# One fused attention and MLP kernel: every queue planned anew with other engine and load times

## The chip, the cores and the metric

The kernel runs on one core of one Trainium2 chip. A core has five instruction queues that matter here: PE (TensorE, the matrix engine, whose weight loads the profile lists apart as PEld), DVE (VectorE), ACT (ScalarE), POOL (GpSimd) and SP (SyncE, which here issues nearly all DMAs). The metric is the device time of one execution in microseconds (us). Before the change the median of three runs was 362.16 us, the lowest 360.83 and the highest 362.58.

## The reference

The first half is a linear attention without a softmax. For each of 8 batches and 8 heads, with 576 positions and 64 features:

```python
kv  = einsum('bhsd,bhse->bhde', k, v)
out = einsum('bhsd,bhde->bhse', q, kv)
rms = sqrt(mean(out*out, axis=-1) + 1e-06)
x   = out / rms * g_norm              # heads side by side: (8, 576, 512)
```

The second half is an MLP block with two mixings, over positions ("tok") and over channels ("ch"), the latter with 2048 hidden units:

```python
a1  = alpha1 * x + beta1
u   = x + lam * einsum('ts,bsd->btd', w_tok, a1)
a2  = alpha2 * u + beta2
out = u + lam * (maximum(a2 @ w_ch1, 0) @ w_ch2)
```

Inputs and output are float32.

## The kernel before

All work is written down as a list of operations and then put in order by a planner inside the kernel file. `P.op(engine, cost, fn, r, w)` notes one operation: its engine (or several engines with a cost for each), a cost in us, the function that issues its instructions, and the keys that it reads and writes, from which dependences follow. Loads and stores are operations of SP with a second figure, `dma_us`, for the transfer.

The stages of one batch b are these, and the names return in the text:

- the product kv(b) on PE: L666 (batch 0 and from batch 2 on), L760 and L770 (batch 1);
- the splitting of q into two bf16 parts (L536 and L621) and its transposition, by PE (L644) for batch 1 and by DMA from batch 2 on; batch 0 is transposed in float32 (L693, L707);
- qkv(b), the second product and its normalisation: L858 for batch 0, L431, L851 and L951 later, then ACT's square (L888), DVE's sum, reciprocal and multiplication (L890, L896, L909), and the input of the next stage, `rt` and, for positions 512 to 575, `rtt` (L915, L981). POOL multiplies x by g for the first two batches (L936, L995);
- tok(b): L1095 for batch 0, L1018, L1049 and L1070 later, then DVE's sum into `xm` (L1031, L1057, L1112);
- ut(b), the transposed input of the channel stage, `a2t`: by PE (L1130) with the evacuations L1139 on ACT and L1140 on DVE for the first two batches, by DMA from batch 2 on;
- ch1(b) on PE (L1181, L1196, L1208 or L1223) with the relu on ACT (L1170, L1171) into `ht`;
- ch2(b) on PE (L1272 and, for the last chunk, L1253), DVE's sum (L1282) and the store.

Beside batches 0 and 1 the weights come in: w_tok is transposed on PE (L1414, L1428), w_ch1 is cast to bf16 and w_ch2 multiplied by lam (L1505). The first loads on SP are chained, so that they are issued in the order in which the program names them.

The planner (`schedule`) simulates five queues. At each moment an idle queue takes the operation of highest priority whose dependences have ended and for which a PSUM bank is free. An operation holds its engine for its cost; what depends on it may start 0.35 us after the end for PE, 0.15 us after it for the others. All loads share one transfer resource (`dma_free`): each takes `dma_us` of it and has landed 2.0 us later. POOL operations and DVE operations marked `port` exclude one another. An operation with costs for two engines goes to the one that would finish it sooner.

As long as the first product of ch1(0) has not started, an idle PE is given fillers: matmuls of zeros (L1586), which keep PE active. Due times are set for the products of ch1(0) and ch2(0) and for the first of ch1(1); `hasten` turns them into priorities for all that these depend on, counted back along the costs. `plan` repeats this for 8 rounds with priorities that are taken backward from the plan before, keeps the best and then shakes its priorities with a list of seeds, each of which moves a random part of them. All other operations keep the priority of their place in the program.

The result is a fixed order on every queue. On the chip nothing is chosen any more: each engine works through its list and waits on semaphores where an operation depends on another queue. The planner's times are not in the program; only the order that follows from them is.

Of the kernel before, what the change touches and what calls it, by code (L numbers as in the profile page):

```python
# [11 lines left out]
ACT = mybir.ActivationFunctionType  # L12
# [37 lines left out]
class Prog:  # L50
# [134 lines left out]
    def schedule(self):  # L185
# [91 lines left out]
        while left:  # L277
            progressed = False
            for e, q in queues.items():
                while q and free[e] <= t + 1e-9:  # L280
                    pick = None
                    first = self.warm and self.warm[0].start is None
                    cands = q[:self.pe_window] if e == "PE" and not first else q[:400]
                    for o in cands:
                        if not ready(o, t):
                            continue
                        if takes_port(o, e) and port_free > t + 1e-9:
                            continue
                        if isinstance(o.eng, tuple) and better_elsewhere(o, e, t):
                            continue  # L290
                        if e in ("ACT", "DVE", "POOL") and sooner(o, e, t):
                            continue
                        pick = o
                        break
                    if pick is None and e == "PE" and first:

                        pick = self.op("PE", 0.43 if t < 6.1 else 0.22, lambda e: self.warm[1](e, self.warm[3]),
                                       r=self.warm[2], w=[self.warm[3]])
                        if ready(pick, t):
                            left += 1  # L300
                            q.append(pick)
                        else:
                            self.ops.remove(pick)
                            self.warm[3].ops.remove(pick)
                            self.lastw.pop(self.warm[3])
                            if self.warm[3].ops:
                                self.lastw[self.warm[3]] = [self.warm[3].ops[-1]]
                            pick = None
                    if pick is None:
                        break  # L310
                    if isinstance(pick.eng, tuple):
                        for e2 in pick.eng:
                            queues[e2].remove(pick)
                        pick.eng, pick.cost = e, pick.cost[e]
                    else:
                        q.remove(pick)
                    for tile in pick.alloc:
                        tile.bank = place(tile, t)
                        for b in range(tile.bank, tile.bank + tile.n):
                            if owner[b] is not None:  # L320
                                pick.deps.update(owner[b].ops)
                            owner[b] = tile
                    pick.start = t
                    free[e] = t + pick.cost
                    if takes_port(pick, e):
                        port_free = free[e]
                    if pick.lat is not None:
                        dma_free = max(dma_free, t + 0.6) + pick.lat
                        pick.end = dma_free + 2.0
                    else:  # L330
                        pick.end = t + pick.cost + (0.35 if e == "PE" else 0.15)
                    order[e].append(pick)
                    events.add(pick.end)
                    events.add(free[e])
                    left -= 1
                    progressed = True
# [100 lines left out]
def bass_transnormer_attn__then__resmlp_affine_kernel(  # L437
# [15 lines left out]
    with ExitStack() as stack:  # L453
# [85 lines left out]
        def load_main(tile, key, src, b, hs, eng="SP"):  # L539
            P.op(eng, 0.6, lambda e: e.dma_start(  # L540
                tile[:, hs].rearrange("p h c d -> p h (c d)"),
                src[b, hs, 0:512, :].rearrange("h (p c) d -> p h (c d)", c=4)),
                w=[(key, a) for a in range(hs.start // 4, hs.stop // 4)],
                dma_us=4.0 * (hs.stop - hs.start) / 8)

        def load_tail(tile, key, src, b, lo, eng="SP"):
            P.op(eng, 0.6, lambda e: e.dma_start(
# [8 lines left out]
        def load_first(a):  # L556
            for key, src, tile in (("kf", k, kf), ("vf", v, vf)):
                P.op("SP", 0.6, lambda e, src=src, tile=tile: e.dma_start(
                    nine(tile, 0, a).rearrange("p x c d -> p x (c d)"),
                    src[0, 4 * a:4 * a + 4].rearrange("(x y) (p c) d -> (y p) x (c d)",  # L560
                                                      y=2, c=9)),
                    w=[(key, a)], dma_us=1.55)

        def load_first_tail(a):
            for y in range(2):
                P.op("SP", 0.45, lambda e, y=y: e.dma_start(
                    qft[0:64, 4 * a + 2 * y:4 * a + 2 * y + 2, :],
                    q[0, 4 * a + y:4 * a + y + 3:2, 512:576, :].rearrange("h s d -> s h d")),
                    w=[("qft0", a, y)], dma_us=0.25)

        def load_kv(b):
            j = (b + 1) % 2
            for tile, src, n in ((kf, k, "kf"), (vf, v, "vf")):
                if b > 1:
                    P.op("SP", 0.6, lambda e, src=src, tile=tile: e.dma_start(
                        tile[:, j].rearrange("p (z f) -> p z f", z=4),
                        src[b].rearrange("(z y) (p c) d -> (y p) z (c d)", y=2, c=9)),
                        w=[(n, j)], dma_us=3.1)
                    continue
                P.op("SP", 0.6, lambda e, tile=tile, src=src: e.dma_start(  # L580
                    rows512(tile).rearrange("p h c d -> p h (c d)"),
                    src[b, :, 0:512, :].rearrange("h (p c) d -> p h (c d)", c=4)),
                    w=[(n, j)], dma_us=3.4)
                for g in range(2):
                    P.op("SP", 0.5, lambda e, tile=tile, src=src, g=g: e.dma_start(
                        rows64(tile)[64 * g:64 * g + 64],
                        src[b, 4 * g:4 * g + 4, 512:576, :].rearrange("h s d -> s h d")),
                        w=[(n + "t", g)], dma_us=0.4)

        def load_q(b, hs=ALL[0], tails=True):  # L590
            load_main(qf, "qf", q, b, hs)
# [32 lines left out]
        def qt_dma(b):  # L624
# [10 lines left out]
            for a, hs in enumerate(HALVES):  # L635
                for cs in PAIRS:
# [3 lines left out]
                    def f(e, cs=cs, t=t, hs=hs, n=n):  # L640
                        for h in range(4):
                            for i, c in enumerate(cs):
# [5 lines left out]
                    P.op("PE", 0.25 * n, f, r=["identb"] + [x for c in cs  # L648
                                                           for x in keys_of(c, (a,))], w=[t])
                    P.op(act_dve(512 * n, 1.5), 0, lambda e, cs=cs, t=t, hs=hs, n=n: copy(  # L650
                        e, qt[:, hs, 128 * cs[0]:128 * cs[0] + 128 * n],
# [91 lines left out]
        def kv_groups(b):  # L743
# [10 lines left out]
            def main(a):  # L754
                ts.append(P.ptile(1))

                def f(e):
# [6 lines left out]
                P.op("PE", 1.1, f, r=[("kf", buf), ("vf", buf)], w=[ts[a]])  # L764

            def tails():
                def f(e):
# [64 lines left out]
        def qkv_groups(b):  # L832

            def group(cs, hs):
# [33 lines left out]
                         + ([("q32", h0 // 2), ("q32", h0 // 2 + 1)] if cs[0] < 4  # L868
                            else [("q32t", h0 // 4)]), w=[t])
                else:  # L870
                    P.op("PE", 0.059 * m + 0.03, f,
                         r=[("qt", c, a) for c in cs for a in aa]
                         + [("kvd", a, h, i) for a in aa for h in range(2) for i in range(3)],
                         w=[t])
# [64 lines left out]
            def tail():  # L939
# [7 lines left out]
                def f(e):  # L947
# [9 lines left out]
                P.op("PE", 0.3, f, r=[("qt", 4, a) for a in range(2)] + KVD, w=[t])  # L957
# [53 lines left out]
        def tok_groups(b):  # L1011
            def group(cs):
                t = P.ptile(len(cs))
                scs = 5 if b < MIX else 4
                for i, c in enumerate(cs):
                    def f(e, i=i, c=c):
                        for sc in range(scs):
                            m = e.matmul(t.ap()[:, i, :], tok_w(sc, c), rsrc(b, sc),  # L1018
                                         start=(sc == 0), stop=(sc == 4))
                        return m  # L1020
                    P.op("PE", 0.217 * scs, f,
                         r=[kk for s in range(scs) for kk in wtk(s) + rkeys(b, s)], w=[t])
                if b < MIX:
                    finish(cs, t)
# [142 lines left out]

        def ch1_groups(b):
            def relu(t, src, dst, fj, n):
                o = P.op("ACT", act_us(n) + 0.09, lambda e: e.activation(  # L1170
                    dst, src(), ACT.Relu, bias=hb[:, fj:fj + 1]) if b > 1 else e.activation(  # L1171
                    dst, src(), ACT.Relu), r=[t, ("hb", fj)] if b > 1 else [t], w=[("ht", fj)])
                mark(b, 0, fj + 1.5, o)
# [195 lines left out]
        for i, hs in enumerate(HALVES):  # L1369
# [4 lines left out]
            wst, moe_w_tok[0:512, :].rearrange("(p c) s -> p c s", c=4)),  # L1374
            w=["wst"], dma_us=3.45)
        P.op("SP", 0.6, lambda e: e.dma_start(wst2, moe_w_tok[512:576, :]),
             w=["wst2"], dma_us=0.6)
        P.chain = False

        wz_op = P.op("DVE", 0.3, lambda e: e.memset(wz.bitcast(mybir.dt.uint32), 0), w=["wz"])  # L1380
# [23 lines left out]
        def wt_groups():  # L1404
# [3 lines left out]
            def group(sc):  # L1408
# [3 lines left out]
                def f(e):  # L1412
# [67 lines left out]
        def load_w(i):  # L1480
# [6 lines left out]
            if i < 4:  # L1487
                P.op("SP", 0.6, lambda e: e.dma_start(
                    s_, moe_w_ch1[:, 512 * i:512 * i + 512].rearrange(
                        "(j p) f -> p j f", p=128)), w=sk, dma_us=2.75)  # L1490
# [95 lines left out]
            return e.matmul(t.flat(), wz[:, 0:128], wz, start=True, stop=True)  # L1586
# [33 lines left out]
```

## Time and profile before

| what | us |
|---|---|
| median of three runs | 362.16 |
| the profiled execution | 360.87 |
| its span, from the first to the last instruction | 359.1 |
| PE busy | 353.5 |
| DVE busy | 239.7 |
| ACT busy | 158.3 |
| POOL busy | 25.9 |
| first product of ch1(0) starts (L1196) | 34.70 |
| first product of ch1(1) starts (L1223) | 78.22 |

The profile shows one execution. Times in its views count from the start of the span. "PE L1272 x28" in a timeline means 28 instructions of line 1272, merged. In the chain that ended last, each step is either work or a wait, named after what ended it. "Busy" means that an instruction was under way on the engine; its successor may start before it ends. The mean granted TensorE clock was 1.000.

### The profile page before, as it was taken

The numbers are of one execution on the slowest core, as the hardware profiler recorded it, in microseconds if no ns is written. First come the engines' busy times: TensorE is split into PE (matmuls) and PEld (weight loads), VectorE is DVE, ScalarE is ACT, GpSimd is POOL, SyncE is SP. The second block draws the span as 40 slices with busy tenths as digits, with TensorE's granted clock in tenths as the row PEclk, the third lists the DMA queues.
The fourth block names the chain that finished last, engine by engine and source line by source line (L and its number), as shares of the span: only waits on it lengthen the run. The fifth ranks groups of instructions, "written<-read, shape, count | busy, mean of one in ns | idle before, by whom it ended". The sixth has DMA issues, their size and how long they took to land.

```text
span 359.1 us, 7676 instructions
## 1 busy us (share of the span) xinstructions
PE 353.5 (98%) x3470; PEld 202.7 (56%) x3246; DVE 239.7 (67%) x356; ACT 158.3 (44%) x274; POOL 25.9 (7%) x31
## 2 busy tenths in 40 slices
PE   8999999989999999999999999999999999999996
PEld 4888464477644654457644654457654554457644
DVE  4388989987884389865995388865996378830021
ACT  2365894047730386018730287017740186007600
POOL 4145024400000000000000000000000000000000
PEclk9999999999999999999999999999999999999999
DMA  7999999599066950589536960387026510140022
GB/s 266 354 356 373 405 409 375 177 230 339 5 88 170 288 203 1 104 149 274 210 79 172 264 235 2 88 157 223 6 58 166 101 31 0 53 131 8 2 58 88
DMA packets 79896, 60.15 MB, mean 168 GB/s; under 512 B 53037, under 2 KB 63541, under 8 KB 79736
## 3 DMA queue, kind: packets, MB, share of 16 engines
q1 hardware_dynamic: 79840, 59.67, 56.9%
q8 instruction: 26, 0.43, 0.5%
q14 instruction: 6, 0.05, 0.0%
q10 hardware_dynamic: 24, 0.01, 0.0%
HBM read 38.82 MB, written 9.44 MB: 134 GB/s over the span
## 4 chain that ended last, share of the span: by engine, by line
PE 97%; DMA 1%; DVE 1%; SPq 0%; issue 0%
PE ps L1272 34%; PE ps L1223 20%; PE ps L1181 15%; PE ps L1018 7%; PE ps L666 5%; PE ps L851 2%; PE ps L431 2%; PE ps L858 1%; PE ps L1049 1%; DMA vf<-in_v_dram 1%; PE ps L1095 1%; PE ps L693 1%; PE ps L1253 1%; PE ps L1130 1%; PE ps L1070 1%; PE ps L951 1%
## 5 line engine op out<-in xcount | busy, mean ns | idle before, releaser
L1272 PE MATMUL ps<-w,ht 128*128 128x512 bf16 x560 | 126.1, 379 | 0.0
L1170 ACT ACTIVATE ht<-ps,hb 128x512 bf16<-128x512 f32 (+1 forms) x96 | 70.9, 740 | 43.2 <-PE ps L1223 33.6
L1272 PEld LDWEIGHTS ps<-w,ht 128*128 128x128 bf16 x560 | 53.2, 98 | 63.1 <-issue 2.0
L1223 PE MATMUL ps<-a2t,w 128*128 128x320 bf16 (+1 forms) x512 | 72.6, 299 | 1.0 <-DVE a2t L1140 1.0
L1223 PEld LDWEIGHTS ps<-a2t,w 128*128 128x128 bf16 x512 | 49.4, 98 | 21.8 <-ACT a2t L1139 1.3
L1181 PE MATMUL ps<-a2t,w 128*128 128x512 bf16 x240 | 54.5, 379 | 0.0
L728 ACT ACTIVATE kvd<-ps 64x128 bf16<-64x128 f32 x24 | 6.5, 272 | 102.8 <-PE ps L666 102.7
L1282 DVE TENSOR_TENSOR xm<-ps,xm 128x512 f32<-128x512 f32 x31 | 21.0, 687 | 26.3 <-PE ps L1272 26.1
L1181 PEld LDWEIGHTS ps<-a2t,w 128*128 128x128 bf16 x240 | 22.6, 98 | 25.4
L890 DVE TENSOR_REDUCE small<-sq 128x16 f32<-128x1024 f32 (+2 forms) x20 | 20.5, 1027 | 18.9 <-ACT sq L888 18.7
L1018 PE MATMUL ps<-rt,wt 128*128 128x512 bf16 x112 | 25.8, 379 | 0.0
L1171 ACT ACTIVATE ht<-ps 128x512 bf16<-128x512 f32 (+1 forms) x32 | 19.9, 653 | 4.5 <-DVE hb L537 2.8
L1031 DVE TENSOR_TENSOR xm<-ps,xm 128x1024 f32<-128x1024 f32 x14 | 17.1, 1220 | 5.4 <-PE ps L1070 5.4
L909 DVE TENSOR_TENSOR xm<-ps,small 128x1024 f32<-128x1024 f32 (+1 forms) x18 | 19.8, 1105 | 0.6
L888 ACT ACTIVATE sq<-ps 128x1024 f32<-128x1024 f32 (+2 forms) x20 | 17.5, 873 | 5.2 <-PE ps L858 3.6
L733 DVE TENSOR_TENSOR kvd<-ps,kvd 64x128 bf16<-64x128 f32 x24 | 6.9, 288 | 18.3 <-ACT kvd L728 18.1
L666 PEld LDWEIGHTS ps<-vf,kf 64*64 64x64 f32 x1008 | 15.9, 135 | 5.3 <-issue 3.4
L1018 PEld LDWEIGHTS ps<-rt,wt 128*128 128x128 bf16 x112 | 10.9, 98 | 12.9 <-issue 0.4
L666 PE MATMUL ps<-vf,kf 64*64 64x64 f32 x1008 | 17.7, 221 | 0.1
L621 DVE TENSOR_TENSOR qs<-qf,qs 128x1024 bf16<-128x1024 f32 x13 | 16.5, 1297 | 0.3 <-ACT qs L536 0.3
L1282 DVE TENSOR_TENSOR xtl<-ps,xtl 128x512 f32<-128x512 f32 x4 | 2.8, 691 | 20.2 <-PE ps L1272 20.1
L1037 DVE TENSOR_TENSOR a2b<-xm,a_bc 128x512 bf16<-128x512 f32 x24 | 15.5, 688 | 0.4
(136 smaller groups left out, 347.1 us busy)
## 6 DMA issues: line engine op xcount, KB each, us to landing
out_dram<-xm SPq DMA_DIRECT2D x31, 256.0 KB, 3.1
qf<-in_q_dram SPq DMA_DIRECT2D x7, 1024.0 KB, 7.2
kf<-in_k_dram SPq DMA_DIRECT2D x6, 1152.0 KB, 7.8
vf<-in_v_dram SPq DMA_DIRECT2D x6, 1152.0 KB, 12.2
stg<-in_moe_w_ch_dram SPq DMA_DIRECT2D x3, 1024.0 KB, 14.5
kf<-in_moe_w_ch_dram SPq DMA_DIRECT2D x2, 1024.0 KB, 12.5
kf<-in_k_dram SPq DMA_DIRECT2D x2, 576.0 KB, 5.1
vf<-in_v_dram SPq DMA_DIRECT2D x2, 576.0 KB, 6.0
```

Source lines behind the costliest of these rows:

```text
L666: m = e.matmul(t.ap(slice(64 * x, 64 * x + 64))[:, y, 0:64], nine(kf, b, a)[r, x, c, :], nine(vf, b, a)[r, x, c, :], start=(c == 0), stop= ...
L888: P.op("ACT", act_us(64 * m), lambda e: e.activation(sqv, raw(), ACT.Square), r=[t], w=[("sq", sqs)])
L890: P.op("DVE", dve_us(64 * m), lambda e: e.tensor_reduce(out=smv, in_=sqv.rearrange("p (h d) -> p h d", h=m), axis=AX.X, op=ALU.add), r=[(" ...
L909: P.op("DVE", dve_us(64 * m), lambda e: e.tensor_tensor(out=x3, in0=split(raw()), in1=inv, op=ALU.mult), r=[t, ("sm", sms)], w=xk, pri=-200)
L1018: m = e.matmul(t.ap()[:, i, :], tok_w(sc, c), rsrc(b, sc), start=(sc == 0), stop=(sc == 4))
L1031: P.op("DVE", dve_us(512 * n), lambda e: e.tensor_tensor(out=x, in0=t.ap(rows) if n > 1 else t.flat(rows), in1=x, op=ALU.add), r=[t] + xk, ...
L1170: o = P.op("ACT", act_us(n) + 0.09, lambda e: e.activation(dst, src(), ACT.Relu, bias=hb[:, fj:fj + 1]) if b > 1 else e.activation(dst, sr ...
L1171: dst, src(), ACT.Relu, bias=hb[:, fj:fj + 1]) if b > 1 else e.activation(
L1181: m = e.matmul(t.flat(), w, a2t[:, dj, 0:512], start=(dj == 0), stop=(dj == 3))
L1223: m = e.matmul(t.ap()[:, i, 0:n], w1[:, dj, 128 * fj:128 * fj + 128], a2t[:, dj, 320 * i:320 * i + n], start=(dj == 0), stop=(dj == 3))
L1272: m = e.matmul(t.flat(), ht[:, fj, 128 * c:128 * c + 128], w2[:, fj, :], start=(fj == 0), stop=(fj == 15))
L1282: P.op("DVE", dve_us(512), lambda e: e.tensor_tensor(out=x, in0=t.flat(), in1=x, op=ALU.add), r=[t] + keys, w=keys)
```

## The change

Only numbers of the planner change, in four kinds: the time after which ACT and DVE are free again, the landing times of loads, the costs of some operations on PE and ACT, and the seeds. What is computed, the engines that may do it and the buffers stay as they are; every queue's order is planned anew from the new numbers.

```diff
 # schedule(): fillers, free times, landings
-  pick = self.op("PE", 0.43 if t < 6.1 else 0.22, lambda e: self.warm[1](e, self.warm[3]),
+  pick = self.op("PE", 0.38 if t < 5.9 else 0.22, lambda e: self.warm[1](e, self.warm[3]),
...
   free[e] = t + pick.cost
+  if e in ("ACT", "DVE") and pick.lat is None:
+      free[e] -= min(0.085, 0.4 * pick.cost)
...
-  pick.end = dma_free + 2.0
+  pick.end = dma_free + 1.75
 # loads: dma_us
-  dma_us=4.0 * (hs.stop - hs.start) / 8)             # q, heads hs
+  dma_us=0.2 + 3.5 * (hs.stop - hs.start) / 8)
-  w=[(key, a)], dma_us=1.55)                         # halves of k and v, batch 0
+  w=[(key, a)], dma_us=1.5)
-  w=[("qft0", a, y)], dma_us=0.25)
+  w=[("qft0", a, y)], dma_us=0.2)
-  w=[(n, j)], dma_us=3.4)                            # k and v, batch 1
+  w=[(n, j)], dma_us=2.9)
-  w=[(n + "t", g)], dma_us=0.4)
+  w=[(n + "t", g)], dma_us=0.3)
-  w=["wst2"], dma_us=0.6)                            # last rows of w_tok
+  w=["wst2"], dma_us=0.7)
-  "(j p) f -> p j f", p=128)), w=sk, dma_us=2.75)    # quarters of w_ch1
+  "(j p) f -> p j f", p=128)), w=sk, dma_us=2.7)
 # costs on PE and of the relu on ACT
-  P.op("PE", 0.25 * n, f, ...)                       # L644, q(1) transposed
+  P.op("PE", 0.225 * n, f, ...)
-  P.op("PE", 1.1, f, ...)                            # L760, kv(1)
+  P.op("PE", 1.02, f, ...)
-  P.op("PE", 0.059 * m + 0.03, f, ...)               # L851, L431, qkv
+  P.op("PE", 0.058 * m, f, ...)
-  P.op("PE", 0.3, f, ...)                            # L951, qkv, last positions
+  P.op("PE", 0.37, f, ...)
-  P.op("PE", 0.217 * scs, f, ...)                    # L1018, tok
+  P.op("PE", 0.222 * scs, f, ...)
-  P.op("PE", 0.65, f, r=rd, w=[t])                   # L1414, w_tok transposed
+  P.op("PE", 0.54, f, r=rd, w=[t])
-  o = P.op("ACT", act_us(n) + 0.09, ...)             # relu
+  o = P.op("ACT", act_us(n) + 0.07 * (b > 1), ...)
 # seeds
-  P.plan(due, 8, (30002, 30023, 30039, 30073, 30134))
+  P.plan(due, 8, (21, 43, 66, 78))
```

More of the change, by code (lines that the diff above doesn't have):

```diff
@@ L647, in f @@
                         return m
-                    P.op("PE", 0.25 * n, f, r=["identb"] + [x for c in cs
+                    P.op("PE", 0.225 * n, f, r=["identb"] + [x for c in cs
                                                            for x in keys_of(c, (a,))], w=[t])
@@ L763, in f @@
                     return m
-                P.op("PE", 1.1, f, r=[("kf", buf), ("vf", buf)], w=[ts[a]])
+                P.op("PE", 1.02, f, r=[("kf", buf), ("vf", buf)], w=[ts[a]])
             def tails():
@@ L870, in group @@
                 else:
-                    P.op("PE", 0.059 * m + 0.03, f,
+                    P.op("PE", 0.058 * m, f,
                          r=[("qt", c, a) for c in cs for a in aa]
@@ L956, in f @@
                     return m
-                P.op("PE", 0.3, f, r=[("qt", 4, a) for a in range(2)] + KVD, w=[t])
+                P.op("PE", 0.37, f, r=[("qt", 4, a) for a in range(2)] + KVD, w=[t])
                 sqv, smv = sq[:, sqs, 0:256], small[:, sms, 0:4]
@@ L1020, in f @@
                         return m
-                    P.op("PE", 0.217 * scs, f,
+                    P.op("PE", 0.222 * scs, f,
                          r=[kk for s in range(scs) for kk in wtk(s) + rkeys(b, s)], w=[t])
@@ L1169, in relu @@
             def relu(t, src, dst, fj, n):
-                o = P.op("ACT", act_us(n) + 0.09, lambda e: e.activation(
+                o = P.op("ACT", act_us(n) + 0.07 * (b > 1), lambda e: e.activation(
                     dst, src(), ACT.Relu, bias=hb[:, fj:fj + 1]) if b > 1 else e.activation(
```

## The prediction

> **What bounds the kernel now.** The page comes first: who is busy, and what the chain that ended last consists of.
>
> ```profile
> span 359.1 us, 7676 instructions
> PE 353.5 (98%) x3470; PEld 202.7 (56%) x3246; DVE 239.7 (67%) x356; ACT 158.3 (44%) x274; POOL 25.9 (7%) x31
> ...
> PE 97%; DMA 1%; DVE 1%; SPq 0%; issue 0%
> ```
>
> TensorE (PE) is the bound. The change leaves every matmul of the computation in place, so it can only remove PE's idle time and its filler matmuls (line 1586, zeros multiplied while PE has nothing ready), or add to them. The chain in order of time shows where these lie (start, length, what):
>
> ```profile
> 1.25 4.73 DMA vf<-in_v_dram
> ...
> 6.03 1.28 PE ps L666 x72
> ...
> 11.20 0.75 PE ps L1586 x3
> 11.95 1.67 PE ps L858 x12
> ...
> 33.28 0.54 PE ps L1586 x2
> ...
> 34.70 1.73 PE ps L1196 x8
> ...
> 59.95 6.15 PE ps L1272 x28
> 66.09 1.08 PE ps L1018 x5
> ...
> 72.58 2.26 PE ps L666 x144
> 74.84 1.69 PE ps L1130 x14
> 76.55 1.54 DVE a2t L1140 x2
> 78.08 0.14 issue
> 78.22 2.34 PE ps L1223 x16
> ```
>
> Until 6.03 PE waits for the first load of v. After that only three things are not the reference's work: 0.75 us of filler at 11.20, 0.54 at 33.28, and a stop of 1.54 at 76.55, before the first product of ch1(1), which waits for the last evacuations of its transposed input. Together 2.83 us, 0.8% of this execution. From 78.22 on the chain is PE to within the last output. The windows view (columns: stretch, then busy us of PE, PEld, DVE, ACT, POOL, then granted clock, DMA share, GB/s) shows which engine could take over as the bound:
>
> ```profile
> 34.70:78.20 43.50, 42.47 (x442) 23.27 (x409) 40.48 (x55) 25.19 (x46) 12.38 (x7) 1.00 0.96 325
> ...
> 80.00:100.00 20.00, 20.00 (x206) 14.09 (x172) 15.97 (x24) 15.59 (x32) 0.00 (x0) 1.00 0.50 167
> ...
> 160.00:320.00 160.00, 160.00 (x1522) 87.27 (x1392) 114.32 (x163) 68.50 (x109) 0.00 (x0) 1.00 0.47 125
> ```
>
> Between 34.70 and 78.20 DVE is busy 40.5 of 43.5 us: nearly a second bound. After 80 it has 20 to 29% free and PE never stops. The due times and the shaken priorities concern only ancestors of the marked products, which all lie in the first 78 us. So I count on no change behind 78.22, and what can move is the first 78 us, whose floor is 78.22 less 2.83, about 75.4.
>
> **The change part by part.** No instruction of the reference's work is added or removed, and no DMA either. What changes is the planner's belief, and through it the order on each queue.
>
> *Landings.* Landing is issue time plus the figure shown.
>
> ```profile
> L558 SPq DMA_DIRECT2D vf<-in_v_dram x1: 454/454/454, 1.2 to 1.2; - x1
> ...
> DMA to landing us min/median/max: 4.7/4.7/4.7
> ...
> L1373 SPq DMA_DIRECT2D ht<-in_moe_w_tok_dram x1: 672/672/672, 7.2 to 7.2; - x1
> ...
> DMA to landing us min/median/max: 10.2/10.2/10.2
> ...
> L1488 SPq DMA_DIRECT2D ht<-in_moe_w_ch_dram x1: 605/605/605, 20.4 to 20.4; - x1
> ...
> DMA to landing us min/median/max: 6.8/6.8/6.8
> ```
>
> v landed at 5.98, w_tok at 17.4, the first quarter of w_ch1 at 27.2. Adding the code's load costs along the chain of SP gives, with the old constants, about 6.55, 18.4 and 30.1; with the new, 6.2, 17.6 and 28.0. The old plan believed loads late by 0.6, 1 and 3 us; the new one by 0.2 to 0.8, and still not early, so a PE that waits for a load which was planned too soon is not to be expected. SP's first loads are chained in a fixed order, so SP issues them as before; what can move on SP and POOL is stores, transposes and the products with g, none of which PE waits for in the chain above.
>
> *Filler before the first product.* The first filler starts at 1.2 in both. 13 of them at the new 0.38 reach 6.14; the planned landing is 6.20, so a fourteenth fits in, where the old figures (0.43 and 6.55) gave 13.
>
> ```profile
> 1.19 4.77 PE L1586 MATMUL ps<-a2b 128*128 128x512 bf16 x13 [1.19 <-DVE eps L1381]
> ...
> 11.24 0.22 ACT L536 ACTIVATE g_bc<-ps 128x64 f32<-128x64 f32 x1
> ...
> 32.49 0.78 ACT L1139 ACTIVATE a2t<-ps,ab 128x512 bf16<-128x512 f32 x1 [3.51 <-PE ps L1130]
> ```
>
> The 13 end at 5.96; one more (0.75/3 = 0.25) ends at 6.21 and holds the product that starts at 6.03. Between 0 and +0.25; I take +0.2.
>
> *The three fillers at 11.20.* L858 needs the last ACT copy, which ends at 11.46; the third filler keeps PE until 11.95. Between 0 and -0.5; I take half, -0.25, since what stands ahead of 11.46 is latency that no order removes.
>
> *The two fillers at 33.28.* PE waits there for DVE's sum into xm. ACT had idled 3.51 us before 32.49 with q(1) already on its way in behind the 27.2 landing, because the old plan had it land later; with the new one its casts can start in that gap and give PE transposes (L644) as work. They share ACT and DVE with the urgent path. Between 0 and -0.54; I take -0.3.
>
> *The stop at 76.55.* Tok(1) (L1018) starts at 66.09, behind 6.15 us of ch2(0) (L1272). DVE's rows say when its last input was ready:
>
> ```profile
> 62.66 1.45 DVE L981 TENSOR_TENSOR rtt<-xtl,e1g_bc 64x512 bf16<-64x512 f32 x1
> 64.14 1.65 DVE L1546 TENSOR_TENSOR lam_bc<-stg,lam_bc 128x512 f32<-128x512 f32 x1
> 65.71 3.42 DVE L621 TENSOR_TENSOR qs<-qf,qs 128x1024 bf16<-128x1024 f32 x2
> ...
> 69.77 1.29 DVE L1282 TENSOR_TENSOR xm<-ps,xm 128x512 f32<-128x512 f32 x2
> ...
> 72.10 0.68 DVE L1282 TENSOR_TENSOR xm<-ps,xm 128x512 f32<-128x512 f32 x1
> ```
>
> rtt is complete at 64.11, so tok(1) could run 1.98 us earlier, with two of the ch2(0) groups kept for the time in which PE now stands. 1.98 is more than 1.54, so the whole stop can go; the L621 of q(2), 4 us of DVE that nobody needs before the third batch, must then give way to the sums behind tok(1). Between 0 and -1.54; a planner that expects DVE and loads when they come has the reason to do this, and I take -1.54. Next late is then the evacuation itself, covered by those two ch2 groups (1.73 us); without that cover the 1.54 is back.
>
> *Engine free times.* ACT and DVE now count as free up to 0.085 us before an operation ends. The rows agree for some kinds: two L1282 take 1.29 where one takes 0.68, an overlap of 0.07. They disagree for others:
>
> ```profile
> 36.48 1.08 DVE L795 COPY kvd<-kvd 64x256 bf16<-64x256 bf16 x4
> ...
> 42.63 7.24 DVE L1505 TENSOR_TENSOR w<-stg,lam_bc 128x1024 bf16<-128x1024 f32 x6
> ...
> L1505 DVE TENSOR_TENSOR w<-stg,lam_bc x6: 1215/1218/1225, 42.6 to 48.7; 128x1024 bf16<-128x1024 f32 x6
> ```
>
> Six L1505 of 1.218 need 7.24, an overlap of 0.01; four L795 start 0.29 apart where the new cost lets the engine go after 0.135. Of the 55 DVE operations up to 78.2 I take half not to overlap: 27 x 0.085 = 2.3 us by which DVE comes later than the new plan has it. The bounds are 0 and 55 x 0.085 = 4.7. Of the 2.3 the 1.98 of slack at tok(1) covers all but 0.3, which I add. The Trainium skill ("Vector Engine (DVE) Microarchitecture Reference", 5.2 Measured stream behaviour on trn2) states 1.0417 ns per column and some 75 ns per instruction once instructions overlap in the queue, an estimate of 1.14 us for 1024 columns. By that rule L1505 would overlap by 0.075 and the 0.3 would be nothing; the row of L1505 does not agree, and I keep the row.
>
> *PE costs.* Only beliefs again, against the chain:
>
> ```profile
> 27.28 2.02 PE ps L760 x64
> ...
> 45.14 0.45 PE ps L644 x8
> ...
> 59.57 0.37 PE ps L951 x16
> ...
> 99.97 3.45 PE ps L1018 x16
> ```
>
> New costs are 2 x 1.02, 0.45, 0.37 and 4 x 0.888 = 3.55: three fit where the old (2.2, 0.5, 0.3) did not, and the fourth moves away from 3.45 (the old gave 3.47). Worth nothing by themselves: PE runs in order and takes what time it takes.
>
> **The sum.** +0.2 - 0.25 - 0.3 - 1.54 + 0.3 = -1.6 us. The profiled execution took 360.87 us (span 359.1 and 1.8 around it), so it would take 359.3. It lies 1.29 below the median of 362.16; on the median's scale the forecast is 360.6, -0.4%.
>
> **The rivals.** *All idle goes* (faster). PE gets no filler after 6.03 and no stop: 2.83 off, 359.3. For it: the ACT gap of 3.51 and tok's slack of 1.98 exceed what they have to cover. Against it: the latency before 11.46, and a fourteenth filler at the start.
>
> *The plan doesn't reach the chip's gaps* (no change). The stop moves, for example to tok(1), which then stands for rtt, or the orders differ only where PE has cover: 0 to -0.3, 362.0. For it: DVE's 40.5 of 43.5 us leave little to rearrange. Also, L981, L1546 and the first L621 ran long while POOL multiplied xm (L981 1.45, where L1282 of a like size takes 0.68), and no cost in the diff speaks of that.
>
> *DVE's plan is too short* (slower). The planner seeks the earliest start of ch1(1), so it may use up the 1.98 of slack and set PE's order tight against DVE's planned times. If then no operation overlaps, DVE is 4.7 late at 78, and the stop at the head of ch1(1) is 4.7 in place of 1.54: +3.2, less 0.35 for the fillers, +2.8, or 365.0. It decides (over 0.5% slower, 1.8 us) from a lateness of 1.54 + 0.35 + 1.8 = 3.7 us, 44 of 55 operations without overlap. For it: L1505 and L795. Against it: L1282. The Trainium skill ("VectorE: DVE Perf Modes", The DRAIN you can't avoid) states that the next operation does not start until the pipe has emptied, which by itself would give this rival's 365.0. The rows of L1282 do not agree with it, those of L1505 do.
>
> **How the numbers follow.** About 0.5% (1.8 us) is what a measurement of this kernel tells from no change. Forecast 0.42, its own range 359.8 to 361.6, of which 0.18 lies beyond -0.5% (below 360.35) and 0.24 within; all idle goes 0.18; no change 0.12; slower 0.28. Faster 0.18 + 0.18 = 0.36, same 0.24 + 0.12 = 0.36, slower 0.28. The range runs from 359.0, just under the case without idle, to 365.0, the slow rival's price.
>
> **What would show it.** In the chain: the DVE step before the first L1223 is gone or under 0.3 us, and L1272 groups stand between tok(1) and the transposes; L1018 starts soon after rtt. In ACT's timeline: casts of q(1) in the gap before 32.5. Fillers: 14 before the first L666, fewer than 5 after. DVE gaps between like operations stay as they are. The prediction is wrong if PE shows new waits on DVE or ACT between 34 and 80, or if idle appears behind 80, where I count on none.

## The result, and the profile after

The changed kernel takes 363.45 us in the median of 13 runs (362.78 to 364.41), the kernel before 361.94 in 13 runs (360.83 to 362.58). The ratio is 1.0045, with an interval of 1.0035 to 1.0056: about 1.6 us slower. The profiled execution took 362.91 us, with a span of 361.1, where that of before took 360.87 and 359.1. The lines of code behind the added two lie two further down (L1272 is now L1274).

The page of the kernel after, with the lines that answer to those of before:

```profile
span 361.1 us, 7665 instructions
PE 353.9 (98%) x3470; PEld 202.9 (56%) x3246; DVE 241.0 (67%) x358; ACT 160.2 (44%) x275; POOL 23.2 (6%) x28
...
PE 91%; DVE 8%; issue 0%
```

PE's busy time has grown by 0.4 us and the span by 2.0, so most of the loss is PE standing. DVE's share of the chain has gone from 1% to 8%. The windows view of the stretch behind the first product of ch1(1), first of the kernel after, then of the kernel before (columns as in the prediction), shows where the loss is not:

```profile
80.31:361.10 280.79, 277.53 (x2583) 154.26 (x2390) 178.06 (x261) 117.83 (x196) 0.00 (x0) 1.00 0.45 122
```

```profile
78.22:359.10 280.88, 277.58 (x2582) 154.31 (x2390) 177.51 (x259) 117.61 (x194) 0.00 (x0) 1.00 0.46 122
```

280.79 against 280.88 us: all of it is in the head, which has grown by 2.09. The chain of the kernel after, in order of time:

```profile
1.19 5.29 PE ps L1588 x14
6.48 1.21 PE ps L668 x72
...
11.27 0.75 PE ps L1588 x3
...
32.82 1.13 DVE qs L623
...
33.99 2.25 DVE qs L539
...
36.27 0.82 DVE a2t L1142
...
37.13 1.04 PE ps L1198 x4
...
68.83 2.88 DVE qs L623 x2
71.71 0.61 DVE xm L1284
...
72.37 2.33 PE ps L1020 x10
...
77.21 1.90 PE ps L1132 x16
79.11 1.21 PE ps L668 x72
80.31 2.29 PE ps L1225 x16
```

The stop of before, ahead of the first product of ch1(1) (now L1225), is gone: PE runs up to it without a step of DVE. Two others have come, and PE's waits name them:

```profile
PE ps L1020 <- DVE xm L1284: 1.6, 1, 1.6
PE ps L1198 <- DVE a2t L1142: 1.2, 1, 1.2
```

The first (35.96 to 37.13) stands before the second half of the first ch1(0) group, for an evacuation of its transposed input. The second (70.80 to 72.37) stands inside tok(1), before the last two of its four L1020 groups, for the sum of a ch2(0) chunk that must free a PSUM bank. In both, DVE had the data and the operation queued, but was inside something else. The timelines of DVE and then POOL in the kernel after (start, busy time, what):

```profile
33.99 2.25 DVE L539 CAST qs<-qft 64x512 bf16<-64x512 f32 x1
64.93 1.76 DVE L1548 TENSOR_TENSOR lam_bc<-stg,lam_bc 128x512 f32<-128x512 f32 x1
67.22 3.90 DVE L623 TENSOR_TENSOR qs<-qf,qs 128x1024 bf16<-128x1024 f32 x2
```

```profile
32.90 3.05 POOL L623 TENSOR_TENSOR qs<-qf,qs 128x1024 bf16<-128x1024 f32 x1 [1.97 <-DVE qs L539]
66.22 3.81 POOL L938 TENSOR_TENSOR xm<-xm,g_bc 128x512 f32<-128x512 f32 x2
```

POOL takes up its L623 at 32.90, as soon as the cast before it has ended. The cast on DVE, 0.42 us when alone (below), ends at 36.24, 0.29 behind the end of POOL's operation, and L1142 stands behind it. The two L623 on DVE take 3.90 where they take 2.52 with POOL held (below). With the multiplications by g they make a row of four, 66.22 to 71.12: 4.90 us, where POOL's two at 1.27 and DVE's two at 1.22 sum to 4.98. They ran one after the other. Ahead of them L1548 takes 1.76 and L983 1.07, where they take 0.68 and 0.69 with POOL held: in all DVE comes 2.8 us later here, of which 1.57 reaches PE.

### The profile page after: what moved, and what is told of

Same layout as the page of the kernel before. It is cut to its first block, busy times and chain, and to the rows that moved or that the text cites. A ratio compares the mean times of both kernels' runs of the same rounds, so it can differ in the third digit from the quotient of the medians.

```text
span 361.1 us, 7665 instructions
## 1 busy us (share of the span) xinstructions
PE 353.9 (98%) x3470; PEld 202.9 (56%) x3246; DVE 241.0 (67%) x358; ACT 160.2 (44%) x275; POOL 23.2 (6%) x28
## 4 chain that ended last, share of the span: by engine, by line
PE 91%; DVE 8%; issue 0%
PE ps L1274 30%; PE ps L1225 19%; PE ps L1183 14%; PE ps L1020 6%; PE ps L668 5%; PE ps L853 2%; PE ps L1588 2%; PE ps L433 2%; PE ps L860 1%; PE ps L1097 1%; DVE qs L623 1%; DVE w L1507 1%; PE ps L1051 1%; PE ps L695 1%; PE ps L1255 1%; PE ps L1072 1%
## 5 line engine op out<-in xcount | busy, mean ns | idle before, releaser
L1274 PE MATMUL ps<-w,ht 128*128 128x512 bf16 x560 | 126.0, 379 | 0.0
L1274 PEld LDWEIGHTS ps<-w,ht 128*128 128x128 bf16 x560 | 53.3, 98 | 63.7 <-issue 2.4
L1225 PE MATMUL ps<-a2t,w 128*128 128x320 bf16 (+1 forms) x512 | 72.7, 299 | 0.0
L1225 PEld LDWEIGHTS ps<-a2t,w 128*128 128x128 bf16 x512 | 49.4, 98 | 20.6 <-ACT ht L1173 0.2
L1284 DVE TENSOR_TENSOR xm<-ps,xm 128x512 f32<-128x512 f32 x31 | 20.8, 686 | 28.6 <-PE ps L1274 28.5
L1020 PE MATMUL ps<-rt,wt 128*128 128x512 bf16 x112 | 25.8, 379 | 1.6 <-DVE xm L1284 1.6
L1020 PEld LDWEIGHTS ps<-rt,wt 128*128 128x128 bf16 x112 | 10.9, 98 | 14.6 <-DVE xm L1284 2.1
L623 DVE TENSOR_TENSOR qs<-qf,qs 128x1024 bf16<-128x1024 f32 x13 | 17.0, 1333 | 0.0
L1284 DVE TENSOR_TENSOR xtl<-ps,xtl 128x512 f32<-128x512 f32 x4 | 2.8, 692 | 20.2 <-PE ps L1274 20.1
```

The costliest lines, as they stand in the source:

```text
L623: lambda e, hi=hi, lo=lo, src=src: e.tensor_tensor(out=lo, in0=src, in1=hi, op=ALU.subtract), r=kin + kh, w=kl, port=True)
L1020: m = e.matmul(t.ap()[:, i, :], tok_w(sc, c), rsrc(b, sc), start=(sc == 0), stop=(sc == 4))
L1225: m = e.matmul(t.ap()[:, i, 0:n], w1[:, dj, 128 * fj:128 * fj + 128], a2t[:, dj, 320 * i:320 * i + n], start=(dj == 0), stop=(dj == 3))
L1274: m = e.matmul(t.flat(), ht[:, fj, 128 * c:128 * c + 128], w2[:, fj, :], start=(fj == 0), stop=(fj == 15))
L1284: P.op("DVE", dve_us(512), lambda e: e.tensor_tensor(out=x, in0=t.flat(), in1=x, op=ALU.add), r=[t] + keys, w=keys)
```

## The experiments

Three theories were set against each other. *Collision*: POOL's operations get between DVE's at moments at which the plan has them apart, because nothing in the program keeps POOL behind DVE. *Lateness*: the new free times make DVE's plan too short, so PE's order is too tight; this is the slow rival of the prediction. *Fillers*: the loss is at the start of the program. In the expectations they are theories A, B and F. Each ratio is to runs of the kernel before that were made together with the run. Where an experiment adds lines, the line numbers of the profile move by four (after) or by as many as the edit has.

**POOL held to the plan, in the kernel after.** In `synchronize()`, which places the waits behind the planning, a POOL operation also waits for the last DVE operation marked `port` that the plan puts ahead of it. No queue's order changes.

```diff
 # synchronize(): for each operation o, in the order of the plan
+if e == "DVE" and o.port:
+    port = o
+if e == "POOL" and port is not None:
+    o.deps.add(port)
```

> The changed kernel, and one rule more: every POOL operation waits for the last DVE operation marked port that the plan places ahead of it, so that POOL can't start earlier than planned and share the port with it. No operation changes its place on its queue. Theory A (the two new stops of PE, 1.17 us at 35.96 and 1.57 us at 70.8, come from DVE operations that POOL slows: the cast of 2.25 us at 33.99 and the two L623 of 3.90 us at 67.22): both stops nearly go, the cast falls to about 0.4 us and the two L623 to 2.4, and the time falls by about 2.5 us against the changed kernel, to 361.0, some 1 us below the kernel before. Theory B (DVE is late because its operations overlap less than the new free time assumes): the cast and the L623 may shorten, but the stops stay within 0.5 us and the time within 0.7 us of 363.45.

360.15 us, a ratio to before of 0.9956 (0.9941 to 0.9972), and a span of 358.1. The timelines of DVE and POOL in this kernel:

```profile
33.71 0.42 DVE L543 CAST qs<-qft 64x512 bf16<-64x512 f32 x1
62.91 0.68 DVE L1552 TENSOR_TENSOR lam_bc<-stg,lam_bc 128x512 f32<-128x512 f32 x1
64.64 2.52 DVE L627 TENSOR_TENSOR qs<-qf,qs 128x1024 bf16<-128x1024 f32 x2
```

```profile
34.22 2.13 POOL L627 TENSOR_TENSOR qs<-qf,qs 128x1024 bf16<-128x1024 f32 x1 [3.44 <-DVE qs L543]
```

POOL's L627 now waits for the cast. The cast takes 0.42 in place of 2.25, the two L627 on DVE take 2.52 in place of 3.90, and POOL's own operation 2.13 in place of 3.05. The rule holds POOL alone: DVE's first L627 still starts while a product on POOL runs to 64.95. The two take 2.52 there, and 2.35 in the kernel before with POOL held, where nothing on POOL stands beside them. In PE's waits between the first product and 85 us nothing over 0.2 is left:

```profile
PE ps L1202 <- ACT a2t L1145: 0.2, 1, 0.2
PE ps L1592 <- issue: 0.2, 1, 0.2
```

The free times of the change are still in this kernel, so lateness by them is not what cost. With the wait added, the change makes the kernel faster than before, by 1.6 us: this version beats both kernels.

**The same rule for one place at a time.** Once only for POOL's part of q(1), once only for the products with g of batch 1.

```diff
 # q1_held
-if e == "POOL" and port is not None:
+if e == "POOL" and port is not None and 30.0 < o.start < 50.0:
 # g_held
-if e == "POOL" and port is not None:
+if e == "POOL" and port is not None and 50.0 < o.start < 80.0:
```

> The changed kernel with the waiting rule for POOL between 30 and 50 us of the plan alone, which is the one product L623 of q(1). Theory A: the DVE cast at 34 us takes about 0.4 us, L1142 runs at about 34.7, PE's stop of 1.17 before the second half of L1198 goes, the stop at 70.8 stays as it is: -1.0 us, 362.4. Theory B: no change beyond 0.3 us.

> The changed kernel with the waiting rule for POOL between 50 and 80 us of the plan alone, which is the products with g of batch 1 (L938, L997). Theory A: the two L623 take 2.4 us, the PSUM bank for tok(1) comes free about 1.5 us earlier, and of the stop of 1.57 before L1020 less than 0.3 is left; the stop at 35.96 stays: -1.4 us, 362.0. It could give some of this back, because the products with g come later and the second L1033 needs them. Theory B: no change beyond 0.3 us.

With q(1) held: 362.01, ratio 1.0008 (0.9999 to 1.0017). With g held: 362.44, ratio 1.0004 (0.9994 to 1.0015). PE's waits on DVE, of the first and then of the second kernel:

```profile
PE ps L1024 <- DVE xm L1288: 1.6, 1, 1.6
```

```profile
PE ps L1202 <- DVE a2t L1146: 1.2, 1, 1.2
```

Each part takes away its own stop and leaves the other. Against the 1.0045 of the kernel after, the parts gain 0.37% and 0.41%, together 0.78%, where the whole rule gains 0.89%: by the intervals the same.

**The rule in the kernel before.** The same four lines, old plan.

> The kernel before with the same waiting rule for all of POOL. There L981, L1546 and the first L621 ran long beside POOL, 2.8 us of DVE in all, ahead of the stop of 1.54 at 76.55. Theory A: the stop shrinks by 0.5 to 1.5 us, 361.0. Theory B, or if the stop there hangs on the evacuations alone: no change beyond 0.3 us of 361.94.

361.95, ratio 1.0001 (0.9993 to 1.0010). DVE's timeline and the chain of this kernel:

```profile
66.99 1.29 DVE L1286 TENSOR_TENSOR xm<-ps,xm 128x512 f32<-128x512 f32 x2
```

```profile
74.87 1.70 PE ps L1134 x14
76.58 1.54 DVE a2t L1144 x2
```

DVE reaches the two L1286 2.8 us earlier than in the kernel before (69.77 there), since nothing holds up L985, L1550 and the L625. The stop ahead of ch1(1) stays as long as it was, 1.54 in the chain: here PE's written order sets it, and DVE's lateness was hidden. So the collision was there before too, and cost nothing: the same 2.8 us of DVE as in the kernel after, of which none reached PE. It costs where the order is so tight that PE comes for just the operation that is held up.

**Fewer first fillers.** The held kernel with 11 in place of 14 fillers before the first product, taken out after the planning.

```diff
+gone = [o for o in P.sequence if P.warm[3] in o.tiles and o.start < 6.5][11:]
+for o in gone:
+    P.sequence.remove(o)
+for o in P.sequence:
+    o.deps.difference_update(gone)
```

> The changed kernel with POOL held back to its planned place, and with 11 instead of 14 fillers ahead of the first product; nothing else moves. In five profiles the block of 14 (or 13) fillers took between 4.43 and 6.03 us, by how soon the fillers shorten, while v lands near 6.0. If the block holds the first product (theory F), three fillers less, at 0.22 to 0.43 each, let it start at the landing, near 6.0, in every run: -0.3 to -0.6 us against 360.15, with less spread. The rival: the fillers are what shortens the products behind them, and with fewer the first products run long: +0.3 or more. If the block is hidden by the load in most runs: within 0.15.

360.20, ratio 0.9942 (0.9930 to 0.9953), against 0.9956 (0.9941 to 0.9972) with 14: the intervals overlap, so it is open whether the last three cost anything. The first row of PE's timeline in the profiled execution: 11 fillers took nearly as long as 14 had. The 72 products behind them took 1.56 us, where they took 1.28 behind 14: what the expectation's rival said, in one execution, and without a loss in the time.

```profile
1.19 4.88 PE L1592 MATMUL ps<-a2b 128*128 128x512 bf16 x11 [1.19 <-DVE eps L1387]
```

**The held kernel without the free times.**

```diff
-if e in ("ACT", "DVE") and pick.lat is None:
-    free[e] -= min(0.085, 0.4 * pick.cost)
```

> The changed kernel with POOL held back, and ACT and DVE free again only when an operation has ended, as in the kernel before; all other new numbers stay. If the new free time is what makes the order good (theory G), its gain goes: 361.5 to 362. If the free time is only an optimism that costs (theory B), this is the faster one: 359.5. If the draw of the seeds decides (theory C): 360.2 give or take 0.5, since the seeds are the same.

365.43, ratio 1.0097 (1.0074 to 1.0119): slower by more than the kernel after, and than any of the three theories expected. With the longer DVE costs the planner finds PE idle before ch1(0) and fills it; PE's timeline:

```profile
33.89 1.03 PE L1590 MATMUL ps<-a2b 128*128 128x512 bf16 x4
```

The trace has 28 fillers in all, against 18 in the kernel after. Lateness would have made this the safer plan, and it is the worse one; whether the free times help by themselves is not shown, since another shaken plan wins without them. In the profiled execution (364.82, 3.95 more than that of before) the way from the first product to the first of ch1(1) takes 74.27 us, 2.08 more than before, and nearly all of the rest is a stop of 1.80, ending at 207.54, that the profile puts down to nothing (last section).

**The held kernel with the old seeds, and with the old landings.** Each goes back to one part of the kernel before: the list of seeds, or all `dma_us` figures and the 2.0.

```diff
 # held_old_seeds
-P.plan(due, 8, (21, 43, 66, 78))
+P.plan(due, 8, (30002, 30023, 30039, 30073, 30134))
```
```diff
 # held_old_landings
-pick.end = dma_free + 1.75
+pick.end = dma_free + 2.0
...
-dma_us=2.9)
+dma_us=3.4)        # and the others as before
```

> The changed kernel with POOL held back, and with the five seeds of the kernel before. Theory C (the draw decides): the gain goes, 361.5 or more. Theory G (the new times make the order good, whatever the seeds): 360.2 to 360.7.

> The changed kernel with POOL held back, and with all landing figures of the kernel before. If the earlier landings are what lets q(1) be split in time (my prediction's step on the fillers at 33.28 and on the stop at 76.55), a good part of the gain goes: 361 to 361.7, with ACT idle again before 32 us. If they do nothing: 360.2 give or take 0.3.

363.00, ratio 1.0023 (1.0014 to 1.0033), and 362.48, ratio 1.0004 (0.9993 to 1.0016). PE's waits, first with the old seeds, then with the old landings:

```profile
PE ps L1229 <- DVE a2t L1146: 1.1, 1, 1.1
```

```profile
PE ps L1229 <- DVE a2t L1146: 1.2, 1, 1.2
```

In both the stop ahead of ch1(1) is back, at its old place. With the old landings ACT idles 2.92 us before 31.62, as expected, and the gain that goes is larger than expected. Neither makes the good order without the other. Since any of them also changes which shaken plan wins, what each is worth by itself can't be read from these runs.

**The kernel after with the old seeds, without the rule.**

```diff
-P.plan(due, 8, (21, 43, 66, 78))
+P.plan(due, 8, (30002, 30023, 30039, 30073, 30134))
```

> The changed kernel with the five seeds of the kernel before, and POOL not held back. With POOL held back this order took 363.0. If what POOL costs depends on how tight the order is set against DVE, this one loses by the collision too, 0.5 to 3 us: 364 to 366. If POOL's collisions hurt only in the order that the four new seeds give: 363.0 give or take 0.3.

365.12, ratio 1.0095 (1.0065 to 1.0124), against 1.0023 with the rule: the collision costs this other order 0.7%, or 2.6 us. PE's waits and DVE's timeline:

```profile
PE ps L1132 <- DVE xtl L1059: 2.3, 1, 2.3
PE ps L1225 <- DVE a2t L1142: 1.1, 1, 1.1
```

```profile
66.44 4.50 DVE L623 TENSOR_TENSOR qs<-qf,qs 128x1024 bf16<-128x1024 f32 x2
```

The same two L623 are held up (they take 2.35 with the rule), here before another consumer, and the first of the two stops is absent with the rule. The collision is thus no accident of one draw of seeds.

**Tok(1) earlier, by hand, in the old order.** This is the prediction's own step done alone: behind the planning, five tok(1) operations of PE move ahead of the last four ch2(0) groups, with their sums on DVE, and the second half of kv(2) ahead of the first. Once without the rule for POOL, once with it.

```diff
 # numbers are operations of the plan; each list goes behind the last number
+P.reorder((("PE", (286, 289, 287, 292, 290), 323), ("PE", (349,), 356),
+           ("DVE", (288, 291, 293, 347, 337, 357), 307)))
```

> The kernel before with one move in its written order: the five groups of tok(1) on PE go ahead of the last four groups of ch2(0), the second half of kv(2) ahead of the first, and on DVE the sums of tok(1) ahead of the three last sums of ch2(0). This is the step of my prediction on the stop at 76.55, done by hand. If that step was right (tok(1) could run 1.98 us earlier and four groups of ch2(0), 3.45 us, then cover the evacuations), PE's stop before the first L1223 falls from 1.54 to under 0.3 and the time by 1.2 to 1.5 us, to 360.6. The rival: DVE, which is still slowed by POOL there until 66.9, is late for the sums, and the stop returns before kv(2) or the transposes: within 0.5 of 362.

> The same move, and POOL held back to its planned place as well. Holding POOL alone gained nothing in the kernel before (1.0001), with DVE's operations 2.8 us earlier and PE's order unchanged. If order and collision are two conditions that have to be met together, this one gains at least what the move alone gains, and 0.3 to 1 us more where the move alone is held up by DVE: 360.3. If POOL never matters in the old order: the same as the move alone.

363.60, ratio 1.0041 (1.0025 to 1.0058); with the rule 362.65, ratio 1.0011 (0.9997 to 1.0025). The expected gain did not come: the first is slower than before. Without the rule PE also waits 0.64 us for `rtt`, whose last part takes DVE 1.44 us where it takes 0.69 with the rule. The chain of the second, up to the first product of ch1(1), and PE's wait there:

```profile
75.36 0.27 ACT kvd L757
...
77.91 1.53 DVE a2t L1169 x2
...
79.58 2.34 PE ps L1252 x16
```

```profile
PE ps L1252 <- DVE a2t L1169: 1.6, 1, 1.6
```

DVE's step in the chain is as long as before, 1.53, and PE's idle time there is 1.56, where it was 1.05 in the kernel before. Tok(1) may come as early as it likes: the transposes (L1159) are still the last work on PE ahead of ch1(1), and their evacuations have nothing beside them on PE. The ch2(0) groups that were kept stand in the wrong place.

**Half of kv(2) behind the transposes.** The same as the last with the rule, with the second half of kv(2) behind the transposes, and on ACT the two copies of that half behind the evacuations.

```diff
-("PE", (349,), 356),
+("PE", (349,), 324), ("ACT", (350, 351), 325),
```

> The kernel before with tok(1) early and POOL held back, and one move more: the second half of kv(2) on PE goes behind the transposes of ut(1), and its two copies on ACT behind the evacuations. In the run without this move the stop before the first L1223 stayed (1.53, with ACT's copies of kv(2) ahead of its evacuations), although four groups of ch2(0) stood between tok(1) and the transposes. If what counts is work of PE behind the transposes, where the order of the changed kernel has half of kv(2), the stop falls under 0.5 and the time by 1.5 to 2.3 us, to 360.3 to 361.1. The rival: the evacuations themselves take so long that half of kv(2), 1.2 us, only moves the stop: within 0.6 us of 362.65.

361.88, ratio 0.9995 (0.9982 to 1.0007). PE's waits:

```profile
PE ps L1252 <- DVE a2t L1169: 0.4, 1, 0.4
PE ps L695 <- DVE xm L1311: 0.3, 1, 0.3
```

The stop falls from 1.56 to 0.35, and one of 0.32 comes, for a PSUM bank. Two things were moved, on PE and on ACT, so the fall belongs to both together. Against the kernel with the wrong place the ratio falls by 0.16% (0.6 us, smaller than expected, and the intervals overlap). The rule has a price of its own in this order: DVE's first sum of tok(1) waits 1.38 us for a product with g that POOL now makes later, and the chain runs over it to the stop of 0.32. The place is the one that the planner found; the chain of the held kernel after (first experiment):

```profile
72.64 1.21 PE ps L672 x72
73.85 1.90 PE ps L1136 x16
75.75 1.21 PE ps L672 x72
76.96 2.29 PE ps L1229 x16
```

Half of kv(2) stands between the transposes and ch1(1), 1.21 us of PE work while the last evacuations run. The kernel after has the same four groups from 76.00 on.

**The head in one table.** The time from the first product (L666 of before) to the first of ch1(1), from PE's timelines, leaves out the first fillers, which differ between executions:

| kernel | first product | ch1(1) | between | less before | ratio of the runs |
|---|---|---|---|---|---|
| before | 6.03 | 78.22 | 72.19 | | |
| after | 6.41 | 80.25 | 73.84 | +1.65 | 1.0045 |
| after, POOL held | 6.12 | 76.89 | 70.77 | -1.42 | 0.9956 |
| only q(1) held | 6.80 | 79.28 | 72.48 | +0.29 | 1.0008 |
| only g held | 7.15 | 79.25 | 72.10 | -0.09 | 1.0004 |
| before, POOL held | 5.99 | 78.25 | 72.26 | +0.07 | 1.0001 |

The ratios, times 362, are +1.6, -1.6, +0.3, +0.1 and 0.0 us: the runs of these kernels follow this stretch within 0.25 us. In the other variants, whose orders move work across the start of ch1(1) or have other fillers, the two differ by up to 1.4 us, so there the ratio alone decides.

## Why the prediction was wrong

The forecast was 359.3 for the profiled execution, 1.6 less than before; it took 362.91, 2.0 more. Point by point:

- *No change behind 78.22*: right, 280.79 against 280.88 us.
- *Landings*: right. No PE wait for a load is new, and ACT's cast of q(1) now stands in the gap ahead of 32.5, as ACT's timeline of the kernel after shows:

```profile
29.67 1.06 ACT L538 ACTIVATE qs<-qf 128x1024 bf16<-128x1024 f32 x1 [0.68 <-DMA qf<-in_q_dram]
```

- *Filler before the first product*: 14, as worked out. +0.2 was taken, with bounds of 0 and 0.25; the profile has +0.45 (6.48 against 6.03). But the same 14 took 5.00 to 6.03 us in other executions, and the 13 of the old order took 4.43 to 5.37, so it can't be read as the price of the fourteenth, and the head without them accounts for the ratio of the runs.
- *The three fillers at 11.20*: -0.25 was taken; all three are still there, 0.75 us. Nothing.
- *The two fillers at 33.28*: -0.3 was taken. One is left. From its start to that of the next work it takes 0.23 us (34.26 to 34.49), where the two took 0.44 (33.22 to 33.66 in PE's timeline; the 0.54 of the chain counts the end of the last one, under which the next work already runs): -0.21.

```profile
34.26 0.39 PE L1588 MATMUL ps<-a2b 128*128 128x512 bf16 x1
```

- *The stop at 76.55*: it went, as said, but by another means and for a smaller sum. The prediction wanted two ch2(0) groups kept behind an earlier tok(1); the hand-made order, with four groups, shows that this leaves the stop in place. It shrinks once half of kv(2) stands behind the transposes, with ACT's copies moved too. And the 1.54 was the length of the two evacuations in the chain, beside the first of which PE still ran transposes: PE's idle time was 1.05, as PE's timeline of the kernel before has it in brackets. So -1.05 in place of -1.54.

```profile
78.22 2.34 PE L1223 MATMUL ps<-a2t,w 128*128 128x320 bf16 x16 [1.05 <-DVE a2t L1140]
```

- *Engine free times*: +0.3 was taken for DVE's lateness. With POOL held and the free times left in, PE has no stop over 0.2: nothing. (The sum also used the 1.98 of slack twice, for an earlier tok(1) and to cover this lateness.) The slow rival, which built on this, came nearest in sign and not in cause.
- **The step that failed** is a sentence in the second rival: L981, L1546 and the first L621 "ran long while POOL multiplied xm", and "no cost in the diff speaks of that". The row was seen, and it got no term in the sum: the collision was held to be something that stays as it is. In the new order it stood in front of two operations that PE was waiting for, 1.17 and 1.57 us, together 2.74 where the sum had nothing.

The sum by what the profile showed is +0.45 - 0.21 - 1.05 + 1.17 + 1.57 = +1.93 of the 2.09 by which the head grew; 0.16 stay unassigned. Without the two stops and the first fillers it is -1.26, and the held kernel's head is 1.42 shorter than that of before. The gain that was forecast, -0.4%, was in the plan, and the held kernel's ratio of 0.9956 has it. That the two agree so closely is in part luck: of the terms, -0.25 and +0.3 came to nothing, and -1.54 to -1.05. The prediction's own sign of failure, new PE waits on DVE between 34 and 80, is what came.

That the collision is the cause of the two stops is shown: holding one place takes away one stop, holding all takes away both. That half of kv(2) behind the transposes took away the stop of before is shown less cleanly. What the fourteenth filler costs, and what each kind of number is worth alone, stays open.

## What to carry to other kernels

A planner that excludes two engines from each other only does so on paper: if the exclusion is part of the plan, the program needs a wait that keeps it, here four lines that took the changed kernel from 1.0045 to 0.9956. When a profile shows operations that run long beside another engine, give that a term in the sum even if the change doesn't touch it, because a new order decides which consumer stands behind them. And a stop for the evacuation of the last work before a stage shrank here when work was placed between the two, and not when work was placed earlier.

## What the runs showed of the hardware

- In these operations DVE and POOL don't run side by side, one waits for the other's whole operation. POOL's L623 is shown from 32.90, while DVE's ran to 33.96, and ended at 35.95: 1.99 behind DVE's end, where it takes 2.13 alone. DVE's cast then lasted 2.25, to 0.29 behind POOL's end, where it takes 0.42. An L1284 with one operand in PSUM kept its 0.68 beside POOL's L938:

```profile
66.61 0.68 DVE L1284 TENSOR_TENSOR xm<-ps,xm 128x512 f32<-128x512 f32 x1
```

  The Trainium skill ("SBUF — State Buffer", SBUF: two separate sides) calls the shared pair of ports an exclusive lock: whichever starts first has it for the whole instruction and the other blocks, for DVE operations in a two-port mode or with two operands in SBUF. The traces agree, with the alternation of 66.22 to 71.12 and with the L1284.
- The same 14 fillers took 5.00, 5.29, 5.68 and 6.03 us in four executions of one order on PE. The groups of PE by line over the first fillers, of the kernel after and of the one with g held, have the mean of one as their last figure before the bar:

```profile
L1588 PE MATMUL ps<-a2b 128*128 128x512 bf16 x14 | 5.3, 560 | 1.2 <-DVE eps L1383 1.2
```

```profile
L1592 PE MATMUL ps<-a2b 128*128 128x512 bf16 x14 | 6.0, 623 | 1.2 <-DVE eps L1387 1.2
```

  560 and 623 ns, and 545 for the 13 of the kernel before. The granted clock reads 1.00 in these stretches, so the profile does not say why. The Trainium skill ("TensorE: Matmul & The Clock Gate", Part 1: The HAM clock gate) reports, for matmuls before the clock has come up, means of 617 and 426 ns in two runs of one kernel. The spread here is alike; no run shows that it is the same thing.
- In some executions PE stands once between 205 and 209 us, with nothing in the profile that releases it: 0.61 us with q(1) held, 0.80 with g held, 1.80 without the free times, 0.33 to 0.71 in four others, and nothing over 0.2 in the kernels before and after and in the one with all of POOL held. PE's timeline with g held:

```profile
208.24 0.19 PE L437 MATMUL ps<-kvd,qt 128*128 128x64 bf16 x1 [0.80 <-issue]
```

  The traces point to a cause that no run tested. Ahead of each of these stops they have one packet of 16 KB on the queue that the page lists as "q8 instruction", and PE goes on 1.2 to 1.4 us after its end: 206.63 and 207.96 with q(1) held, 206.81 and 208.24 with g held, 206.17 and 207.54 without the free times. In the kernel after it ended at 205.40, and PE, 2.2 us later, came to the qkv products of this place at 207.58 without a stop. So PE seems to wait there for its own instructions, though no row says whose the packet's are. It is one reason why the head was compared by itself above, and not the spans of single executions.
